# Key rows for the memory by DMA transposes of two fp16 halves, and memory products two row groups later

## The chip, the cores and the metric

One core of a Trainium2 chip runs the kernel. The metric is device microseconds of one execution, the median of three runs. The core has TensorE (PE, with weight loads as PEld), VectorE (DVE), ScalarE (ACT), GpSimd (POOL), and SyncE (SP), whose queue issues all DMAs of this kernel.

## The reference

A gated sum of an attention branch with a memory and a GeGLU feed-forward branch, over one sequence of 2048 rows of 576 numbers (32 heads of 18). The attention branch goes through four segments of 512 rows; each reads a memory that the earlier segments' keys and values built up:

```python
phi = lambda t: jnp.where(t > 0, t + 1.0, jnp.exp(t))
...
for s in range(N):
    qs, ks, vs = q[:, :, s], k[:, :, s], v[:, :, s]
    logits = jnp.einsum("bhqd,bhkd->bhqk", qs, ks) * scale + mask
    a_dot = jnp.einsum("bhqk,bhkd->bhqd", _softmax(logits), vs)
    pq = phi(qs)
    num = jnp.einsum("bhld,bhde->bhle", pq, M)
    den = jnp.einsum("bhld,bhd->bhl", pq, z)[..., None] + 1e-6
    outs.append(g * num / den + (1.0 - g) * a_dot)
    pk = phi(ks)
    M = M + jnp.einsum("bhld,bhle->bhde", pk, vs)
    z = z + jnp.einsum("bhld->bhd", pk)
...
b = (gelu(x @ w_gate) * (x @ w_up)) @ w_down
return gx * (o @ wo) + (1 - gx) * b
```

The change touches only the lines of M and z: how phi(k), computed with columns in the partitions, gets its rows (tokens) into the partitions for the product with v.

## The kernel before

Numbers are carried as pairs of fp16, a high half and the low rest, and products are sums of three half products. The program has two parts. The first, up to about 208 us, makes q, k and v for the four segments, the gate and the memory; the second interleaves the feed-forward branch with the attention heads and ends with the output product. The change lies in the first part.

Segment s (0 to 3) consists of **row groups** (s from 1 on; four groups q of 128 tokens) and nine **column products** j (`project`; j 0 to 3 queries, 4 shared by queries and keys, 5 to 8 keys; 128 columns by 512 tokens each). p = s - 1 is the segment whose keys are put into the memory while s runs.

A row group makes v of 128 tokens in two halves (`vrows`, then `put_rows`: ACT writes the high half of `vstage`, DVE the low one), and, between them, calls `key_rows(p, q - 1)`. From segment 2 on it ends with `recall` (queries times memory, in the two `st` banks of PSUM; `put_recall` on DVE frees them), and then with `memorize(p, q - 1)`, fifteen small products into the banks `U` and `pv`. Group 3's `key_rows` comes after the last group, its `memorize` after column product 0, and `keep_memory` folds the sum into `bd` at column product 1.

A column product is put away by `put_columns` one step later: ACT writes the high half of `stage`, then Relu and Exp into `expm`; DVE makes `phi` from PSUM, POOL adds `expm`; DVE makes the low half of `stage`, and SP writes both to DRAM. The columns of j = 8 are put away in row group 0 of the next segment. Beside j = 5 to 8, `next_x` makes the fp16 halves of the next segment's x (`high_x` on ACT, L205; `low_x` on DVE, L210 and L215).

`key_rows` turns 128 tokens of the five key blocks of `phi` (four blocks into one bank, L714, the fifth into bank `V`, L715) by TensorE transposes against an fp32 identity; ACT scales the result from PSUM into the high half of `krow` (L720), and DVE makes the low half (L724).

PE, ACT, DVE and POOL run in the order in which the code calls them; `finish_later` sends out work that a helper has put into the list `later`. SP's queue is set in order by the framework, by the place of each DMA's data, and SP waits in order too. The buffers of a pool (`stage` 4, `expm` 2, `phi` 9, `vstage` 6) come free when their last reader is done.

Of the kernel before, what the change touches and what calls it, by code (L numbers as in the profile page):

```python
# [45 lines left out]
def kernel(ctx: ExitStack, tc: tile.TileContext, xs, wqk, wv, wo, wgu, wd, beta, out):  # L46
# [472 lines left out]
    kmc = cst.tile([P, 3, 4], F32, name="kmc")  # L519
# [6 lines left out]
    with tc.tile_pool(name="prj", bufs=2, side="right", reuse_waits="tile") as pp:  # L526
# [10 lines left out]
        W, phi, vst, kr, mem = {}, {}, {}, {}, {}  # L537
# [15 lines left out]
        def square_sum(o, r, on_act):  # L553
            if on_act:
                junk = flat(pa.tile([P, 2, KT * P], F16, name="kjunk", bufs=1)).bitcast(BF16)
                act.activation(junk[:, : r.shape[1]], r, AF.Square, accum_out=o)
            else:
                sum_squares(o, r)
# [22 lines left out]
        later, held = [], []  # L581
# [31 lines left out]
        def put_columns(s, j, pr):  # L613
            hf, c = divmod(s, 2)
            st = pp.tile([P, 2, L], F16, name="stage", bufs=4)
# [4 lines left out]
            if with_phi:  # L620
                e = pp.tile([P, L], F32, name="expm", bufs=2)
                f = phi[s, j] = pp.tile([P, L], F32, name="phi", bufs=9)
                act.activation(e, pr, AF.Relu, scale=nal[:, s, i // 2 : i // 2 + 1])
                act.activation(e, e, AF.Exp, scale=-1.0)

            def rest():
                if with_phi:
                    dve.tensor_scalar(f, pr, al[:, s, i : i + 1], 0.0, OP.mult, OP.max)
                    (dve if j == 8 and s == 0 else pool).tensor_tensor(f, f, e, OP.add)
                if j < 8 or s == 3:  # L630
                    words()
# [9 lines left out]
        def put_rows(s, q, b, pv, unit, a):  # L641
# [3 lines left out]
            if b == 0:  # L645
                st = vst[s, q] = pa.tile([P, H, VC], F16, name="vstage", bufs=6)
# [62 lines left out]
        def key_rows(s, q):  # L709
            ka, kb = bank("G") if s else bank("st", 2), bank("V")  # L710
            tok = slice(q * P, (q + 1) * P)

            for i in range(4):
                pe.transpose(ka[:, i * P : (i + 1) * P], phi[s, 4 + i][:, tok], ident)  # L714
            pe.transpose(kb[:, :P], phi[s, 8][:, tok], ident)  # L715
            k = kr[s, q] = krow[q % 2]
            sc = kmc[:, s, 1:2]
            parts = (slice(0, 448), ka[:, 64:]), (slice(448, D), kb[:, :P])
            for o, r in parts:
                act.activation(k[:, 0, o], r, AF.Copy, scale=sc)  # L720

            def low():
                for o, r in parts:
                    dve.scalar_tensor_tensor(k[:, 1, o], r, sc, k[:, 0, o], OP.mult, OP.subtract)  # L724

            later.append(low)

# [1101 lines left out]
```

## Time and profile before

| what | value |
|---|---|
| median of 3 runs | 1556.35 us (1556.0 to 1557.39) |
| the profiled execution, first to last instruction | 1553.8 us |
| granted TensorE clock, mean | 1.000 |
| first part, to the first feed-forward product | about 208 us |
| row groups of segments 1, 2, 3 begin at | 51.3, 98.8, 150.9 us |
| column products of segments 1, 2, 3 begin at | 70.2, 122.5, 174.8 us |

The profile gives the span of the profiled execution only; the runs were timed without it, and their median lies 2.55 us above that span. Rows of a timeline read: start in us, length in us, engine, line, operation, what is written <- what is read, shapes, count, and in brackets how long the engine stood idle before and who released it. Rows of stretches give the busy time of PE, PEld, DVE, ACT and POOL in that order, then TensorE's granted clock, the share of DMA engines busy, and GB/s.

### The profile page before, as it was taken

To read this page: it belongs to the slowest core of one execution; us is meant where nothing else is said; L and a number is where in the kernel's file an instruction comes from. 1 tells how busy PE (TensorE), PEld (TensorE's weight loads), DVE (VectorE), ACT (ScalarE), POOL (GpSimd) and SP (SyncE) were. 2 spreads that over 40 slices of the span, in tenths; PEclk is the share of its full clock that TensorE was granted. 3 is DMA by queue.
4 is the path that set the end of the run, shared out by engine and by line. 5 is a ranking of instruction groups with operands and counts; after the bars stand their busy time and mean duration, and the time that the engine had idled before them with its cause. 6 is when DMAs were issued, how large, how long until landed. Compare 5 with 4: busy or idle time off the path is not lost.

```text
span 1553.8 us, 33925 instructions
## 1 busy us (share of the span) xinstructions
PE 1548.4 (100%) x12195; PEld 955.7 (62%) x12196; DVE 1229.3 (79%) x3198; ACT 1183.7 (76%) x2037; POOL 1305.8 (84%) x1313
## 2 busy tenths in 40 slices
PE   9999999999999999999999999999999999999999
PEld 5665655666666566666666665666666666666577
DVE  6788976778878887878788887878787878887665
ACT  7567544888888888888888888888888888876421
POOL 3544778899898999989899989898999989899597
PEclk9999999999999999999999999999999999999999
DMA  7533341667768687778777878878687878774654
GB/s 254 195 127 125 132 150 34 122 126 140 133 131 141 130 144 130 144 126 137 132 136 126 140 139 136 135 140 151 127 138 133 144 128 141 130 136 99 120 118 138
DMA packets 472601, 210.14 MB, mean 135 GB/s; under 512 B 427632, under 2 KB 437360, under 8 KB 471920
## 3 DMA queue, kind: packets, MB, share of 16 engines
q1 hardware_dynamic: 472432, 207.97, 67.6%
q8 instruction: 96, 1.57, 0.4%
q14 instruction: 73, 0.60, 0.1%
HBM read 92.03 MB, written 27.26 MB: 77 GB/s over the span
## 4 chain that ended last, share of the span: by engine, by line
PE 94%; POOL 3%; ACT 2%; DVE 1%; issue 1%; POOLq 0%
PE dn L1228 27%; PE U L1268 22%; PE V L1268 12%; PE pv L1183 4%; PE G L385 3%; PE st L447 3%; PE dn L454 2%; PE U L1275 2%; PE dn L385 1%; PE U L447 1%; PE V L1280 1%; PE G L1280 1%; PE st L1137 1%; PE G L447 1%; PE st L1669 1%; PE V L1275 1%
## 5 line engine op out<-in xcount | busy, mean ns | idle before, releaser
L1228 PE MATMUL dn<-paird,hh 128*128 128x288 f16 x3396 | 476.5, 286 | 0.2
L1164 POOL TENSOR_TENSOR pf<-pf,ph 128x512 f16<-128x512 f32 (+1 forms) x256 | 359.2, 1403 | 94.6 <-ACT ph L1163 83.6
L1228 PEld LDWEIGHTS <-hh 128*128 128x128 f16 x3456 | 332.2, 98 | 139.1 <-issue 18.1
L1268 PEld LDWEIGHTS <-pairg 128*128 128x128 f16 x2616 | 244.0, 98 | 254.8 <-issue 18.3
L1236 DVE SCALAR_TENSOR_TENSOR acc<-dn,ev,acc 128x288 f32<-128x288 f32 x534 | 274.4, 515 | 51.4 <-PE dn L1228 42.9
L1153 ACT ACTIVATE pf<-pf,mb,esc 128x512 f32<-128x512 f32 (+3 forms) x512 | 293.0, 642 | 5.2
L1268 PE MATMUL U<-xt,pairg 128*128 128x512 f16 x864 | 209.9, 379 | 0.2 <-DVE gl L1459 0.2
L1268 PE MATMUL U<-x,pairg 128*128 128x512 f16 x840 | 204.1, 379 | 0.0
L426 POOL TENSOR_TENSOR pairg<-raw,pairg 128x640 f16<-128x640 f32 (+2 forms) x144 | 176.2, 1239 | 3.0 <-ACT pairg L418 1.5
L1163 ACT ACTIVATE ph<-pf 128x512 f16<-128x512 f32 (+1 forms) x256 | 172.4, 720 | 0.0
L1255 POOL TENSOR_TENSOR hh<-gl,hh 128x512 f16<-128x512 f32 x144 | 164.4, 1163 | 7.5 <-ACT hh L1254 7.5
L1140 DVE CUSTOM_DVE_ANT_0 pf<-st,mask 128x512 f32<-128x512 f32 (+1 forms) x256 | 157.2, 614 | 0.0
L418 ACT ACTIVATE pairg<-raw 128x640 f16<-128x640 f32 (+2 forms) x144 | 89.3, 647 | 56.6 <-POOL raw L410 36.2
L1258 ACT ACTIVATE gl<-gl,sc 128x512 f32<-128x512 f32 x144 | 97.2, 716 | 40.7 <-DVE gl L1505 30.1
L303 POOL TENSOR_SCALAR raw<-raw,sc 128x640 f32<-128x640 f32 x72 | 118.7, 1663 | 0.0
L1459 DVE COPY gl<-U 128x512 f32<-128x512 f32 x72 | 49.8, 692 | 85.4 <-PE U L1268 74.9
L1150 ACT ACTIVATE mb<-mx,esc 128x4 f32<-128x4 f32 x128 | 37.5, 293 | 103.4 <-DVE mx L1140 103.4
L1140 DVE CUSTOM_DVE_ANT_0 pf<-dn,mask 128x256 f32<-128x256 f32 (+1 forms) x192 | 67.2, 375 | 55.3 <-PE dn L1137 55.3
L1268 PE MATMUL V<-xt,pairg 128*128 128x512 f16 x432 | 105.7, 381 | 0.0
L1268 PE MATMUL V<-x,pairg 128*128 128x512 f16 x432 | 104.8, 378 | 0.0
L1254 ACT ACTIVATE hh<-gl 128x512 f16<-128x512 f32 x144 | 82.6, 616 | 16.0 <-DVE gl L1250 15.8
L1183 PEld LDWEIGHTS <-pt 128*128 128x128 f16 x2560 | 83.4, 96 | 12.3
(354 smaller groups left out, 2971.1 us busy)
## 6 DMA issues: line engine op xcount, KB each, us to landing
raw<-in_wgu_dram SPq DMA_DIRECT2D x36, 640.0 KB
rawd<-in_wd_dram SPq DMA_DIRECT2D x36, 288.0 KB
qk<-stage SPq DMA_DIRECT2D x36, 256.0 KB
qt<-qk SPq DMA_DIRECT2D x128, 72.0 KB
kt<-qk SPq DMA_DIRECT2D x128, 72.0 KB
vp<-vstage SPq DMA_DIRECT2D x16, 296.0 KB
vt<-vp SPq DMA_DIRECT2D x16, 296.0 KB
qt<-qk SPq DMA_DIRECT2D x128, 36.0 KB
```

Of the source, the lines that this page charges most:

```text
L303: pool.tensor_scalar(r, r, scl[f // 2][0][:, 0:1], None, OP.mult)
L426: pool.tensor_tensor(spot(f, *p, 1), raw_g[f][:, p[0] : p[1]], spot(f, *p, 0), OP.subtract)
L1140: dve.tensor_tensor_reduce(prob[a][:, COL[qi] : COL[qi] + (qi + 1) * P], out[qi], mask[:, L - (qi + 1) * P :], 1.0, -3e38, OP.add, OP.max, ...
L1153: act.activation(r, r, AF.Exp, bias=b[:, qi : qi + 1], scale=esc[:, 0, c : c + 1])
L1163: act.activation(h[:, cols], p[:, cols], AF.Copy)
L1164: pool.tensor_tensor(p.bitcast(F16)[:, cols], p[:, cols], h[:, cols], OP.subtract)
L1183: pe.matmul(ov, pr[:, 10 * i + COL[qi] // P + kb], v[:, 4 * e + kb, c0 : c0 + VC], start=kb == 0 and i == 0, stop=kb == qi and i == 1)
L1228: pe.matmul(o[:, :NH], hh[:, a, q * P : (q + 1) * P], w[:, b, n * NH : (n + 1) * NH], start=i == 0, stop=i == 5)
L1236: dve.scalar_tensor_tensor(av, o[:, :NH], ev, av, OP.mult, OP.add)
L1255: pool.tensor_tensor(hh[:, 1], t, hh[:, 0], OP.subtract)
L1258: act.activation(t, o, AF.Gelu_apprx_tanh, scale=scl[f // 2][0][:, 2 + c : 3 + c])
L1268: pe.matmul(o, w[:, i, (a + k) * P : (a + k + 1) * P], x[:, b + k], start=start and k == 0 and i == 0 and b == h, stop=k == 1 and i == 1, ...
```

## The change

The transposes leave TensorE. `phi` of key columns is scaled by its power of two when it is made (`kmc` columns 2 and 5 as the factor, and columns 3 and 4, its logarithm, as the bias of Exp). For each of the five key blocks of segments 0 to 2, `turn_keys` has ACT copy `phi` to fp16 into the first half of the block's own `expm` buffer, POOL write the rest phi - high into the second half, and SP turn each half by one DMA transpose of 128 (64 for block 4) columns by 512 tokens into `krow`, which now holds all four groups.

```diff
-        def key_rows(s, q):
...
-            for i in range(4):
-                pe.transpose(ka[:, i * P : (i + 1) * P], phi[s, 4 + i][:, tok], ident)
-            pe.transpose(kb[:, :P], phi[s, 8][:, tok], ident)
...
-                act.activation(k[:, 0, o], r, AF.Copy, scale=sc)
...
-                    dve.scalar_tensor_tensor(k[:, 1, o], r, sc, k[:, 0, o], OP.mult, OP.subtract)
+        def turn_keys(at_once=False):
+            while to_turn:
+                s, j, e = to_turn.pop(0)
+                h = slice(64 if j == 4 else 0, P)
+                f, w = phi[s, j], e.bitcast(F16).rearrange("p (i t) -> p i t", i=2)
+                act.copy(w[h, 0], f[h])
+                def low():
+                    pool.tensor_tensor(w[h, 1], f[h], w[h, 0], OP.subtract)
+                    for i in range(2):
+                        sp.dma_start(krow[:, :, i, max(0, (j - 4) * P - 64) : (j - 3) * P - 64], w[h, i], transpose=True)
+                low() if at_once else lows.append(low)
```

In `put_columns` the copy of the block before stands between Relu and Exp, and its subtraction behind the sum of the present block; the sum of block 8 is on DVE in every segment:

```diff
                 act.activation(e, pr, AF.Relu, scale=nal[:, s, i // 2 : i // 2 + 1])
-                act.activation(e, e, AF.Exp, scale=-1.0)
+                turn_keys()
+                if j >= 4 and s <= 2:
+                    act.activation(e, e, AF.Exp, scale=-1.0, bias=kmc[:, s, 4:5] if j == 4 else kmc[:, s, 3:4])
+                else:
+                    act.activation(e, e, AF.Exp, scale=-1.0)
...
-                    (dve if j == 8 and s == 0 else pool).tensor_tensor(f, f, e, OP.add)
+                    (dve if j == 8 else pool).tensor_tensor(f, f, e, OP.add)
+                while lows:
+                    lows.pop(0)()
+                if keys:
+                    to_turn.append((s, j, e))
```

In the row groups and column products:

```diff
                         put_rows(s, q, 0, *pv)
                         if s == 3 and q == 0:
+                            for i in range(2):
+                                squares(0, 1, i, act_square)
+                        turn_keys(True)
+                        if s == 3 and q == 0:
                             norm_x(3, bank("V"))
-                        if q:
-                            key_rows(p, q - 1)
...
-                        if q:
-                            memorize(p, q - 1)
+                        if q > 1:
+                            memorize(p, q - 2)
                     finish_later()
-                    key_rows(p, 3)
...
-                    if s and j == 0:
+                    if s and j < 2:
                         finish_later()
-                        memorize(p, 3)
+                        memorize(p, j + 2)
+                    if j == 2 and s < 3:
+                        key_scale(s)
...
-                    if s and j == 1:
+                    if s and j == 2:
                         keep_memory(p)
```

Besides: `stage` has 3 buffers, `expm` 4, `phi` 8, `vstage` 7; `krow` also serves as scratch for squares and for `keep_memory`; `key_scale` is called at j = 2 of its own segment, with five small instructions more; the POOL scalings `outscale` are called one at j = 5, 6 and 7 each instead of all at j = 4 or 5, and `mix_scale` in segment 2; of the `form_sums` subtractions in the row groups of segments 2 and 3, two and one move from DVE to POOL, and their ACT part comes later in the group.

ACT and DVE at the border of segments 1 and 2, where the last column product of segment 1 is put away and row group 0 of segment 2 runs (`expm`, `stage`, `phi` belong to the column products, `vstage` to the rows of v, `mo` to `put_recall`). Before, ACT:

```order
L618 ACTIVATE stage<-G 128x512
L623 ACTIVATE expm<-G,nal 128x512
L624 ACTIVATE expm<-expm 128x512
L651 ACTIVATE vstage<-dn 128x16x18 x2
L651 ACTIVATE vstage<-U 128x16x18
```

and now:

```order
L632 ACTIVATE stage<-G 128x512
L637 ACTIVATE expm<-G,nal 128x512
L588 CAST expm<-phi 128x512
L640 ACTIVATE expm<-expm,kmc 128x512
L675 ACTIVATE vstage<-dn 128x16x18
L588 CAST expm<-phi 128x512
L675 ACTIVATE vstage<-dn 128x16x18
L675 ACTIVATE vstage<-U 128x16x18
```

The first cast reads `phi` of block 7, the second that of block 8; each now stands ahead of a `vstage`. DVE at the same place now has the sum of block 8 ahead of the first `vstage` and of `put_recall`:

```order
L648 TENSOR_SCALAR phi<-G,kmc 128x512
L649 TENSOR_TENSOR phi<-phi,expm 128x512
L678 SCALAR_TENSOR_TENSOR vstage<-dn,vstage 128x16x18
L658 SCALAR_TENSOR_TENSOR stage<-G,stage 128x512
L678 SCALAR_TENSOR_TENSOR vstage<-dn,vstage 128x16x18
L680 TENSOR_SCALAR gate<-dn,al 128x1
L718 COPY mo<-st 128x19
```

Before, that sum was on POOL. SP's queue from block 4 of segment 0 to the first rows of segment 1 (`qk` and `vp` are written to DRAM, `raw` is read for the x of segment 2). Before:

```order
L635 DMA qk<-stage 128x2x512
L161 DMA raw<-in_xs_dram 128x1024
L635 DMA qk<-stage 128x2x512
L161 DMA raw<-in_xs_dram 128x1024
L657 DMA vp<-vstage 128x1184
L635 DMA qk<-stage 128x2x512
L657 DMA vp<-vstage 128x1184
L635 DMA qk<-stage 128x2x512
```

Now, the second half of the same stretch:

```order
L593 DMA_TRANSPOSE krow<-expm 128x4x128
L681 DMA vp<-vstage 128x1184
L593 DMA_TRANSPOSE krow<-expm 128x4x128 x2
L161 DMA raw<-in_xs_dram 128x1024
L593 DMA_TRANSPOSE krow<-expm 128x4x128 x2
L659 DMA qk<-stage 128x2x512
L681 DMA vp<-vstage 128x1184
```

Ten transposes now stand between these transfers, in the order in which their halves are made; the last two rows of transposes are blocks 7 and 8, with a load of x between them.

More of the change, by code (lines that the diff above doesn't have):

```diff
@@ L6 @@
 from concourse._compat import with_exitstack
-from concourse.masks import make_identity
 F32 = mybir.dt.float32
@@ L753, in keep_memory @@
                 else:
-                    m = flat(pa.tile([P, 2, KT * P], F16, name="kjunk", bufs=1)).bitcast(F32)[: o.shape[0], : o.shape[1]]
+                    o, d, k = (t.rearrange("p (a b) -> p a b", a=2) for t in (o, d, k))
+                    m = krow[: o.shape[0], 0, :, : 2 * o.shape[2]].bitcast(F32)
                     dve.scalar_tensor_tensor(m, o, sm[: o.shape[0]], k, OP.mult, OP.mult)
@@ L795 @@
                 pool.memset(t, 1e-30)
-            krow = [pa.tile([P, 2, KT * P], F16, name=f"krow{i}", bufs=1) for i in range(2)]
-            for t in krow:
-                pool.memset(t[:, :, D:], 0.0)
+            krow = pa.tile([P, 4, 2, KT * P], F16, name="krow", bufs=1)
+            pool.memset(kmc[:64, :, 4:5], 0.0)
             bdm = pa.tile([P, KT, 8 * MC], BF16, name="bdm", bufs=1)
@@ L858, in next_x @@
                         add_squares(c, (3,))
-                if j == (4 if c > 1 else 5):
-                    for i in range(3):
-                        outscale(c, i)
                 if 5 <= j < 8:
@@ L1051 @@
                     finish_later()
+                    if s < 3 and 5 <= j < 8:
+                        outscale(s + 1, j - 5)
                     if (s, j) == (1, 3):
```

75 lines of the change are left out of this document (36 added, 39 removed).

## The prediction

> **What bounds the kernel now.** I read the page first, then who TensorE waited for over the whole run, then the timeline around the transposes. The page's first lines:
>
> ```profile
> span 1553.8 us, 33925 instructions
> PE 1548.4 (100%) x12195; PEld 955.7 (62%) x12196; DVE 1229.3 (79%) x3198; ACT 1183.7 (76%) x2037; POOL 1305.8 (84%) x1313
> ```
>
> TensorE is busy for 1548.4 of 1553.8 us, and the whole list of what it waits for before is three short rows:
>
> ```profile
> PE G L783 <- POOL wst L779: 1.0, 1, 1.0
> PE dn L457 <- DVE wv L128: 0.4, 1, 0.4
> PE U L1268 <- DVE gl L1459: 0.2, 1, 0.2
> ```
>
> So the kernel is TensorE's queue from end to end. An instruction taken off that queue is worth its place in the queue; any new wait of TensorE is lost in full. The sum is therefore (places removed) minus (waits added). I work against the profiled span, 1553.8 us; the median of the runs, 1556.35, is 2.55 us above it, and I carry that difference unchanged.
>
> **What leaves TensorE.** One call of `key_rows`, in segment 1 and row group 1, and behind it a place in the same timeline where one chain of `vrows` follows the other with nothing between:
>
> ```profile
> 56.32 0.29 PE L457 MATMUL U<-wv,x 128*128 128x288 f16 x1
> 56.45 0.60 PE L714 MATMUL st<-ident,phi 128*128 128x128 f32 x4
> 56.88 0.27 PE L715 MATMUL V<-ident,phi 128*128 128x128 f32 x1
> 56.99 1.64 PE L454 MATMUL dn<-wv,x 128*128 128x290 f16 x12
> ...
> 52.88 0.29 PE L457 MATMUL dn<-wv,x 128*128 128x288 f16 x1
> 53.00 1.64 PE L454 MATMUL dn<-wv,x 128*128 128x290 f16 x12
> L715 PE MATMUL V<-ident,phi x12: 272/273/273, 56.9 to 174.7; 128*128 128x128 f32 x12
> ```
>
> Matmuls overlap, so starts count, not durations. From the last matmul of a chain to the first of the next it is 0.67 us with five transposes and 0.12 us without: 0.55 us a call. The last row shows twelve calls (one `kb` transpose each): 12 x 0.55 = **6.6 us removed**. The memory products stay the same fifteen per row group; moving them two groups later changes no count. Nothing waited for these transposes long, so their removal opens no further wait of TensorE.
>
> **What is added, on engines beside TensorE.** Fifteen blocks of key columns (five in each of segments 0 to 2) get one ACT copy to fp16, one POOL subtraction and two DMA transposes. The nearest rows of the same shapes:
>
> ```profile
> L1254 ACT ACTIVATE hh<-gl 128x512 f16<-128x512 f32 x144 | 82.6, 616 | 16.0 <-DVE gl L1250 15.8
> L1255 POOL TENSOR_TENSOR hh<-gl,hh 128x512 f16<-128x512 f32 x144 | 164.4, 1163 | 7.5 <-ACT hh L1254 7.5
> ```
>
> That is 0.6 us on ACT and 1.2 us on POOL a block. ACT and DVE lose the copies and subtractions of `key_rows`, so in sum they are relieved. What matters is where the new work stands: in the ACT queue the copy of block 7 stands between Relu and Exp of block 8, and it waits for POOL's sum of block 7; block 8's own sum is now a DVE instruction that waits for that Exp; and ahead of the next `vstage` on ACT stands the copy of block 8, which waits for that sum. In the rows before of segment 2 these read:
>
> ```profile
> 100.80 1.27 POOL L629 TENSOR_TENSOR phi<-phi,expm 128x512 f32<-128x512 f32 x1 [1.50 <-ACT expm L624]
> ...
> 100.17 0.63 ACT L624 ACTIVATE expm<-expm 128x512 f32<-128x512 f32 x1
> 100.71 0.41 ACT L651 ACTIVATE vstage<-dn 128x288 f16<-128x288 f32 x1
> ...
> 53.85 0.87 DVE L629 TENSOR_TENSOR phi<-phi,expm 128x512 f32<-128x512 f32 x1
> ...
> 103.01 0.45 DVE L654 SCALAR_TENSOR_TENSOR vstage<-dn,vstage 128x288 f16<-128x288 f32 x1
> 103.62 0.18 DVE L694 COPY mo<-st 128x19 f32<-128x19 f32 x1
> 104.96 0.82 DVE L705 TENSOR_TENSOR mo<-st,rden 128x396 f32<-128x396 f32 x2
> ...
> 107.41 1.37 PE L683 MATMUL st<-bd,phi 128*128 128x152 f32 x10
> ```
>
> POOL's sum of block 7 ends at 102.07; before, ACT was through with Exp at 100.8 and did not care. Now: copy 0.6, Exp 0.6, DVE sum 0.87 (the row at 53.85, the one such sum that was on DVE), copy 0.6, `vstage` 0.41, its low half and the gate column 0.6: 105.75. Only then does `put_recall` of group 0 start; it took 103.62 to 105.78, 2.16 us, so it ends near 107.9 and frees both `st` banks. TensorE wants them for the next `recall` at 107.41 - 0.55 = 106.86. **A new wait of 1.0 us** in segment 2.
>
> The same in segment 3, where two squares of `raw` now stand ahead of that copy:
>
> ```profile
> 152.74 1.27 POOL L629 TENSOR_TENSOR phi<-phi,expm 128x512 f32<-128x512 f32 x1 [1.37 <-DVE phi L628]
> ...
> 154.59 0.74 ACT L556 ACTIVATE kjunk<-raw 128x640 bf16<-128x640 f32 x1 [0.57 <-DMA raw<-in_wgu_dram]
> 155.45 0.74 ACT L556 ACTIVATE kjunk<-raw 128x640 bf16<-128x640 f32 x1
> ...
> 157.12 0.17 DVE L694 COPY mo<-st 128x19 f32<-128x19 f32 x1
> 158.45 0.82 DVE L705 TENSOR_TENSOR mo<-st,rden 128x396 f32<-128x396 f32 x2
> ...
> 159.76 1.37 PE L683 MATMUL st<-bd,phi 128*128 128x152 f32 x10
> ```
>
> 154.0 + copy 0.6 + Exp 0.6 + `vstage` 0.4 = 155.6; the two squares 1.6 (154.59 to 156.19 by these rows): 157.2; copy 0.6, `vstage` 0.4, low half and gate 0.6: 158.8; `put_recall` 2.15: 160.95. TensorE comes at 159.76 - 0.55 = 159.2. **A new wait of 1.7 us.** If POOL's sum or `raw` is 1 us later, both waits grow by it; if the earlier blocks run ahead, they vanish. Bounds: 0 to 2.5 us and 0 to 4 us.
>
> **The transposes by DMA** have no row of this size. The nearest are the probability transposes, 128 rows by 1280 against 512 here:
>
> ```profile
> L1169 SPq DMA_TRANSPOSE pt<-ph x128: 1252/1372/3217, 273.6 to 1420.7; - x128
> ...
> 55.75 0.37 SPq L635 DMA_DIRECT2D qk<-stage  x1
> ...
> 44.00:60.00 16.00, 16.00 (x126) 11.61 (x125) 13.98 (x30) 10.71 (x21) 13.69 (x13) 1.00 0.98 315
> 600.00:1000.00 400.00, 400.00 (x3329) 244.26 (x3328) 325.87 (x888) 341.11 (x580) 363.50 (x352) 1.00 0.78 135
> ...
> 51.73 1.27 POOL L629 TENSOR_TENSOR phi<-phi,expm 128x512 f32<-128x512 f32 x1 [1.84 <-DVE phi L628]
> 58.72 0.80 PE L737 MATMUL U<-vstage,krow 128*128 128x152 f16 x9
> 59.68 1.63 PE L454 MATMUL dn<-wv,x 128*128 128x288 f16 x12
> 63.67 0.80 PE L737 MATMUL U<-vstage,krow 128*128 128x152 f16 x9
> ```
>
> One occupies SP's queue for 1.37 us; for 512 columns between 0.55 (in proportion) and 1.37 (fixed); I take 1.0, between them, since nothing here decides. In the two rows of stretches the last column but one is the DMA share: at 600 to 1000 us the engines are 0.78 busy for 135 GB/s, at 44 to 60 us 0.98 busy for 315 GB/s. So traffic with such transposes moves fewer bytes per busy time, 173 GB/s when full; a block's two, 0.26 MB, would then fill the engines for 1.5 us, and those of segment 0 fall into the stretch that is full already. I let a landing be 1 to 4 us. TensorE wants them all, complete, for `memorize(0, 0)` at 63.67 - 1.1 (two calls of `key_rows`) - 0.96 (the memory products that leave group 1, 58.72 to 59.68) = 61.6. Block 7's sum ends at 53.0; copy, Exp and block 8's sum as above give 55.1, its copy 55.7, its subtraction, behind block 7's, about 57.5. Ten transposes and eight plain transfers go through SP from 44 us on: at 1.0 and 0.37 us 13 us, so SP is just through. Two issues and a landing later it is 60.5 to 63.5. **I take a wait of 1.0 us**, bounds 0 to 4. In segments 2 and 3 `recall` gives the transposes 1.2 us more a group: no wait.
>
> **The lock between DVE and POOL** can make all three worse:
>
> ```profile
> 43.60 1.27 DVE L210 SCALAR_TENSOR_TENSOR x<-raw,xsc,x 128x1024 f16<-128x1024 f32 x1
> 95.19 2.01 DVE L210 SCALAR_TENSOR_TENSOR x<-raw,xsc,x 128x1024 f16<-128x1024 f32 x1
> 94.84 1.28 POOL L629 TENSOR_TENSOR phi<-phi,expm 128x512 f32<-128x512 f32 x1 [1.91 <-DVE phi L628]
> ```
>
> The same DVE instruction takes 1.27 us with POOL idle and 2.01 us when POOL is inside a sum that began just before it. The Trainium skill (SBUF — State Buffer, "SBUF: two separate sides") states an exclusive lock on a shared port pair; these rows agree (0.74 us more). Each segment's blocks 4 to 8 now have a second POOL instruction of 1.2 us beside DVE's `low_x`. One collision more, about half an instruction, per segment: 0.5 us, thrice, **1.5 us**, bounds 0 to 3.5.
>
> **Sum.** -6.6 + 1.0 + 1.7 + 1.0 + 1.5 = -1.4 us: span 1552.4, time **1555.0 us**.
>
> **Rivals.** 1. *The waits hide* (faster). POOL's scale instructions of `outscale` are spread out and `expm` has four buffers, so the earlier blocks may run ahead and the ACT chain end in time. Only about 1.5 us of wait remain: 1556.35 - 5.1 = 1551.3. Against it stands DVE (third number, 90 to 102 us), which is busy for 11.87 of 12 us there, so that block 7 cannot come sooner than DVE lets it:
>
> ```profile
> 90.00:102.00 12.00, 12.00 (x69) 6.51 (x68) 11.87 (x16) 9.30 (x16) 6.67 (x8) 1.00 0.62 191
> ```
>
> 2. *The transposes land late* (slower). SP takes its queue in order, and between the transposes stand the writes of `stage` (one buffer fewer) and the loads of x. At 1.37 us an issue, ten make 13.7 us, SP is still issuing at 61 us in segment 0, and every `memorize` of the first groups waits: 4 us in segment 0, and with 1.5 in each later one and the upper bounds of the ACT chain (2.5 and 4) less what overlaps (2): 11.5 - 6.6 = +4.9: 1561.2. It decides when landing comes 4 us after the last subtraction. The Trainium skill (VectorE: DVE Perf Modes, "The three transpose paths") points this way: it gives 390 ns for a 128x128 on TensorE, 1309 ns by DMA, and advises TensorE where PSUM will do. By that price 36 blocks a segment would be 47 us, and TensorE would stand for tens of us. The trace disagrees: here one instruction of ten such blocks leaves SP in 1.37 us, and TensorE's queue, not a transpose's own duration, is what costs.
>
> 3. *The change does not do what it says*: transposes left on TensorE. In the order of the changed program none is left; no chance.
>
> **How the numbers follow.** Near balance, waits between 3.5 and 9.7 us: 0.44. Waits hidden, rival 1: 0.32. Late transposes, rival 2: 0.24. A measurement can tell about 0.2%, 3.1 us, so faster means below 1553.2 and slower above 1559.5. The range leaves out about a tenth at each end: from nearly all of the 6.6 us kept (1550.5) to just short of rival 2's full price (1560.8).
>
> **What would show it.** No L714 or L715 row, and TensorE's chains 0.12 us apart in the row groups. In TensorE's list of waits: `recall` on `put_recall` (DVE) in group 1 of segments 2 and 3, about 1 and 1.7 us; the first `memorize` of segment 1 on a DMA, about 1 us. ACT's copies idle on POOL's `phi`. The prediction is wrong if that list stays below 3 us (then 1551), if a DMA or SP heads it with over 4 us, or if waits appear beyond 205 us, where I expect the same times shifted.

## The result, and the profile after

| | before | after |
|---|---|---|
| median of 5 runs each | 1556.35 us | 1569.84 us |
| ratio of the runs, 95% interval | | 1.0083 [1.0071, 1.0095] |
| profiled execution, first to last instruction | 1553.8 us | 1567.9 us |
| granted TensorE clock, mean | 1.000 | 0.996 |

The change makes the kernel 13.5 us slower. The prediction was 1555.0 us, in a range of 1550.5 to 1560.8. (One execution of the experiment k1 below took 5611.21 us; its median is that of its other four.) The page of the changed kernel:

```profile
span 1567.9 us, 33879 instructions
PE 1548.7 (99%) x12135; PEld 951.4 (61%) x12136; DVE 1228.5 (78%) x3188; ACT 1182.0 (75%) x2028; POOL 1330.6 (85%) x1327
```

TensorE has 60 instructions fewer (twelve calls of five transposes) and is busy no less: 1548.7 against 1548.4 us. Idle are 19.2 us of its span instead of 5.4. The list of what TensorE waits for had three rows; now it reads (us in total, times, longest):

```profile
PE pv L742 <- DMA krow<-expm: 3.0, 1, 3.0
PE dn L99 <- DVE vstage L678: 2.9, 1, 2.9
PE st L707 <- DVE mo L729: 2.4, 2, 1.5
PE dn L454 <- DVE gate L680: 2.0, 2, 1.0
PE dn L454 <- DVE vstage L678: 1.8, 2, 1.2
PE U L742 <- DMA krow<-expm: 1.1, 1, 1.1
PE G L795 <- POOL wst L791: 1.0, 1, 1.0
PE dn L457 <- DVE wv L128: 0.5, 1, 0.5
PE dn L707 <- DVE mo L729: 0.3, 1, 0.3
```

L742 is `memorize`, L707 `recall`, L454 a chain of `vrows`, L99 the column sums of `scales(0)` in segment 3. All but the last three rows are new; of the three, two stood in the list before, and 0.3 us fall at the end of the first part. Where the time goes is read from the first product of each stage of TensorE's timeline (row groups of segment 1, its columns, and so on):

```profile
52.76 1.64 PE L454 MATMUL dn<-wv,x 128*128 128x288 f16 x12 [1.02 <-DVE gate L680]
74.81 1.46 PE L447 MATMUL dn<-x,wp 128*128 128x512 f16 x6
104.38 1.63 PE L454 MATMUL dn<-wv,x 128*128 128x288 f16 x12
128.98 2.32 PE L447 MATMUL dn<-x,wp 128*128 128x512 f16 x10
158.56 1.63 PE L454 MATMUL dn<-wv,x 128*128 128x288 f16 x12
187.45 1.89 PE L447 MATMUL dn<-x,wp 128*128 128x512 f16 x8
```

Before, these stood at 51.29, 70.15, 98.77, 122.49, 150.88 and 174.82. Each segment has four `key_rows` fewer in its rows (2.2 us) and one `memorize` of 0.96 us moved into its columns, so the growth of a stage plus 3.16 us is what its rows lost:

| stage | growth, us | lost in it, us | waits listed there | slower clock (next section) |
|---|---|---|---|---|
| up to the rows of segment 1 | 1.5 | 1.5 | 1.0 | |
| rows of segment 1 | 3.2 | 6.4 | 4.0 | 1.5 |
| rows of segment 2 | 0.9 | 4.0 | 3.3 | |
| rows of segment 3 | 5.0 | 8.1 | 4.7 | 2.9 |
| columns of segments 1 and 2 | 0.9, 1.2 | 0, 0.2 | | |

20.2 lost less 6.6 removed is 13.6 of the 14.1 us. The listed waits and the slower clock are 17.4 of the 20.2. Part of the rest comes from how a wait is listed: from the modelled end of the last product, while products overlap. At the first wait of segment 1 two products start 1.30 us apart (51.46 and 52.76) where 0.12 is usual, so 1.18 us are lost for 1.02 listed. What remains was not traced. Behind 205 us nothing new waits for more than 0.3 us.

### The profile page after: what moved, and what is told of

It is laid out like the page before. It is cut to its first block, busy times and chain, and to the rows that moved or that the text cites. A ratio compares the mean times of both kernels' runs of the same rounds, so it can differ in the third digit from the quotient of the medians.

```text
span 1567.9 us, 33879 instructions
## 1 busy us (share of the span) xinstructions
PE 1548.7 (99%) x12135; PEld 951.4 (61%) x12136; DVE 1228.5 (78%) x3188; ACT 1182.0 (75%) x2028; POOL 1330.6 (85%) x1327
## 4 chain that ended last, share of the span: by engine, by line
PE 88%; POOL 5%; DVE 3%; ACT 2%; issue 1%; DMA 1%; SPq 0%; POOLq 0%; DVEq 0%; ACTq 0%
PE dn L1239 27%; PE U L1279 22%; PE V L1279 12%; PE pv L1194 4%; PE G L385 3%; PE U L1286 2%; PE dn L385 1%; PE st L447 1%; PE G L1291 1%; PE V L1291 1%; PE st L1148 1%; PE st L1680 1%; PE V L1286 1%; PE G L1286 1%; PE dn L454 1%
```

## The experiments

All times are medians beside runs of the kernel before on the same chip (1555.9 to 1556.7 us). The ratios differ from those of the medians by up to 0.0004, so a difference of under 1 us between two experiments decides nothing. Line numbers of an experiment differ from those of the changed kernel by a few.

### Segment 1: the queue of SP, and the clock behind a wait

What TensorE waits for in the rows of segment 1 is issued by SP. In the changed kernel all thirty transposes on SP's queue (min/median/max in ns), POOL's subtraction of block 8, SP's rows around the last transposes of segment 0, TensorE's rows that wait for them, and a chain of segment 3:

```profile
L593 SPq DMA_TRANSPOSE krow<-expm x30: 1177/1214/2406, 44.7 to 172.1; - x30
...
58.54 1.16 POOL L591 TENSOR_TENSOR expm<-phi,expm 128x512 f16<-128x512 f32 x1 [1.10 <-ACT expm L588]
...
58.65 1.23 SPq L593 DMA_TRANSPOSE krow<-expm  x1
59.97 0.53 SPq L681 DMA_DIRECT2D vp<-vstage  x1
60.59 2.53 SPq L593 DMA_TRANSPOSE krow<-expm  x2
63.17 1.14 SPq L161 DMA_DIRECT2D raw<-in_xs_dram  x1
64.40 2.52 SPq L593 DMA_TRANSPOSE krow<-expm  x2
...
65.03 0.60 PE L742 MATMUL U<-vstage,krow 128*128 128x152 f16 x3 [1.05 <-DMA krow<-expm]
68.61 0.91 PE L742 MATMUL pv<-vstage,krow 128*128 128x152 f16 x6 [2.98 <-DMA krow<-expm]
69.33 2.70 PE L454 MATMUL dn<-wv,x 128*128 128x288 f16 x12
...
175.14 2.71 PE L454 MATMUL dn<-wv,x 128*128 128x288 f16 x12
```

SP works through its queue without a gap; the subtraction of block 8 is done at 59.70 (58.54 + 1.16), but its transposes leave only at 64.40. And behind the wait the same twelve products that take 1.63 us elsewhere take 2.70, and 2.71 behind the waits of segment 3. So two theories: SP's time per transpose, and the granted clock.

**one_dma**: one transpose a block for both halves.

```diff
-                    for i in range(2):
-                        sp.dma_start(krow[:, :, i, max(0, (j - 4) * P - 64) : (j - 3) * P - 64], w[h, i], transpose=True)
+                    sp.dma_start(krow.rearrange("p i q c -> p (i q) c")[:, :, max(0, (j - 4) * P - 64) : (j - 3) * P - 64], e.bitcast(F16)[h], transpose=True)
...
-            krow = pa.tile([P, 4, 2, KT * P], F16, name="krow", bufs=1)
+            krow = pa.tile([P, 2, 4, KT * P], F16, name="krow", bufs=1)
```

> One DMA transpose a block for the high and the low half together, 15 instructions instead of 30; the bytes, the casts and the subtractions stay. Theory SP (each transpose holds SP's queue about 1.2 us whatever its size, so ten of them put the last one of segment 0 behind the first memorize of segment 1): the time between the starts of two transposes stays near 1.2 to 1.6 us though each moves twice the columns, the wait of TensorE for krow in the rows of segment 1 (3.0 + 1.1 us in the changed kernel) falls to 0 to 1 us, the slower clock behind it goes too, and the time falls by 3 to 5.5 us, to 1564.5 to 1567 us. Rival DMA (the moving of the bytes is what is late): a transpose of twice the columns takes twice as long on SP's queue or to land, and wait and time stay within 1 us (1569 to 1571 us). In segments 2 and 3 both expect the waits unchanged.

Measured: 1563.53 us, ratio to before 1.0047 [1.0032, 1.0062]; 6.3 us less than the changed kernel (5.6 by the ratios). The wait for `krow` is 1.7 us instead of 4.1, and behind it the clock stays full. (In segment 3, behind pauses of 2.86 and 0.82 us, it still falls: twelve products take 3.08 us there.) Twice the columns hold SP's queue for 1.30 instead of 1.21 us:

```profile
L592 SPq DMA_TRANSPOSE krow<-expm x15: 1194/1303/3062, 50.2 to 165.6; - x15
```

Theory SP holds, the rival DMA falls: the bytes are the same. The wait fell a little less than expected and the gain was a little larger.

**fill**: products that nothing reads, where TensorE waited longest.

```diff
+                        if (s, q) == (1, 2):
+                            o = bank("pv")
+                            for _ in range(22):
+                                pe.matmul(o, onesb, mask, start=True, stop=True)
```

and twelve of them ahead of `scales(0)` in segment 3.

> The changed kernel with matrix products that nothing reads, put where TensorE waits longest: 22 of 128x512 ahead of the first memorize of segment 1, 12 ahead of the column sums of the squares in segment 3 (some 4.7 and 2.6 us at full clock). Theory CLOCK (a wait of about 3 us makes the granted clock fall to half for some us behind it): the granted clock no longer falls behind these two places, the chain that took 2.70 us behind the first of them takes 1.63 again, and the time stays equal or falls by up to 4 us although the fillers add up to 3 us more than the waits that they cover: 1566 to 1570 us. Rival (the clock falls for another reason, as the power of the products before): the chains stay at 2.7 us behind the same products, and the fillers add 2 to 4 us, 1572 to 1574 us.

Measured: 1567.04 us, 1.0066 [1.0051, 1.0081]; 2.8 us less than the changed kernel, with 34 products more. The chains behind the two places:

```profile
68.76 1.63 PE L454 MATMUL dn<-wv,x 128*128 128x288 f16 x12
167.52 1.65 PE L454 MATMUL dn<-wv,x 128*128 128x290 f16 x12 [0.83 <-DVE gate L680]
```

In the changed kernel they took 2.70 and 1.97 us, and in segment 3 the recall and the chain behind took 2.71 each instead of 1.37 and 1.63. So the pauses themselves cost some 1.5 + 2.9 us beyond their length. Theory CLOCK holds.

### Segments 2 and 3: the ring of ACT and POOL

In segment 2 of the changed kernel, POOL, ACT, DVE and TensorE around the start of the row groups at 104.38 (L649 is a sum, L591 the subtraction of a low half, L588 the fp16 copy):

```profile
101.83 2.02 POOL L591 TENSOR_TENSOR expm<-phi,expm 64x512 f16<-64x512 f32 x1
104.20 1.81 POOL L649 TENSOR_TENSOR phi<-phi,expm 128x512 f32<-128x512 f32 x1
105.97 1.16 POOL L591 TENSOR_TENSOR expm<-phi,expm 128x512 f16<-128x512 f32 x1
107.64 1.27 POOL L649 TENSOR_TENSOR phi<-phi,expm 128x512 f32<-128x512 f32 x1
...
106.04 0.62 ACT L588 CAST expm<-phi 128x512 f16<-128x512 f32 x1 [1.28 <-POOL phi L649]
108.95 0.62 ACT L588 CAST expm<-phi 128x512 f16<-128x512 f32 x1 [0.61 <-POOL phi L649]
110.09 0.41 ACT L675 ACTIVATE vstage<-dn 128x288 f16<-128x288 f32 x1
111.73 0.62 ACT L588 CAST expm<-phi 128x512 f16<-128x512 f32 x1 [1.23 <-DVE phi L649]
...
110.22 1.47 DVE L649 TENSOR_TENSOR phi<-phi,expm 128x512 f32<-128x512 f32 x1 [0.67 <-ACT expm L640]
...
112.12 1.64 PE L454 MATMUL dn<-wv,x 128*128 128x290 f16 x12 [1.20 <-DVE vstage L678]
115.48 1.45 PE L707 MATMUL st<-bd,phi 128*128 128x152 f32 x10 [1.48 <-DVE mo L729]
```

The reader is to see a ring. The copy of block 6 waits for POOL's sum of block 6; Exp of block 7 stands behind that copy; the sum of block 7 needs that Exp, and stands on POOL behind the low half of block 5; the copy of block 7 waits again. The first `vstage` begins 5.7 us after the row groups; before it was 1.9 us (100.71 against 98.77).

**cast_behind**: the copies stand behind Exp of the next block, that of block 8 behind both `vstage`. **both**: this and one_dma.

```diff
-                turn_keys()
...
                     act.activation(e, e, AF.Exp, scale=-1.0)
+                turn_keys()
...
-                        turn_keys(True)
...
                         put_rows(s, q, 1, *pv)
+                        turn_keys(True)
```

> The fp16 copies of the key blocks move back in ACT's order: behind Exp of the next block instead of ahead of it, and the one of block 8 behind both vstage copies of row group 0. Theory ACT (the copies wait for POOL's and DVE's sums and hold up the vstage copies behind them): the waits of TensorE for dn and st in segments 2 and 3 (L454, L99, L707: 2.9 + 2.4 + 2.0 + 1.8 us) fall to 2 to 5 us in sum, the clock loss of 3 us in segment 3 goes for the most part, and the time falls by 4 to 8 us; the wait for krow in segment 1 may grow by 1 to 2 us since the transposes start later. Rival LOCK (DVE and POOL instructions lengthened by each other, or the buffers of phi and stage, make the sums late): the same waits stay within 1.5 us in sum, and the time stays at 1568 to 1572 us.

> One transpose a block, and the copies moved back in ACT's order. If SP and ACT are both right and act in different segments, the gains add up: 7 to 13 us less than the changed kernel, 1557 to 1563 us. If SP alone: 1564.5 to 1567. If ACT alone: 1562 to 1566. If neither: 1568 to 1572.

Measured: cast_behind 1568.10 us, 1.0072 [1.0055, 1.0089]; both 1565.36 us, 1.0055 [1.004, 1.007]. The waits of segments 2 and 3 fell only from 8.0 to 6.2 us in cast_behind, less than ACT asked for and a little more than LOCK allowed; the time lies in LOCK's range. With one_dma beneath it the move lost 1.8 us: the waits of segments 2 and 3 fell from 7.0 to 5.3, but since the copies of segment 0 came later too, the wait for `krow` was 3.7 us, against 1.7 in one_dma, and the clock fell behind it. So in both the gain in segments 2 and 3 and the loss in segment 1 hid each other, and its time, which lies where SP alone or ACT alone would put it, shows neither.

**no_low** goes on from one_dma and leaves out the subtraction in segments 1 and 2, so only the high half is transposed there; **no_keys** leaves out the copies and transposes as well.

```diff
+                    if s:
+                        sp.dma_start(krow[:, 0, :, max(0, (j - 4) * P - 64) : (j - 3) * P - 64], w[h, 0], transpose=True)
+                        return
                     pool.tensor_tensor(w[h, 1], f[h], w[h, 0], OP.subtract)
...
                 s, j, e = to_turn.pop(0)
+                if s:
+                    continue
```

The first addition is no_low's, the second stands only in no_keys.

> One transpose a block as in one_dma (1563.5 us), and in segments 1 and 2 the subtraction that makes the low half is left out (ten POOL instructions of 1.16 to 2.03 us; the products with the low half read old values), so only the high half is transposed there. Theory POOL (its queue, with each low half ahead of the next block's sum, makes the sums late for which ACT and DVE wait): the waits of TensorE in segments 2 and 3 (1.8 + 1.5 + 2.9 + 0.8 us in one_dma) fall to 0 to 3 us, the clock loss of about 3 us in segment 3 goes, and the time falls by 5 to 9 us, to 1554.5 to 1558.5 us. Rival ACT (the copies in its order are enough): these waits stay within 1.5 us in sum, the time within 2 us.

> As no_low, and in segments 1 and 2 the fp16 copies on ACT and the transposes are left out too (the memory products read the keys of segment 0 again); what stays of the change there is the sum of block 8 on DVE, the scale columns, and the later memory products. Theory POOL: nothing more to gain than no_low gains, within 1.5 us. Rival ACT: the time falls by 6 to 10 us against one_dma, to 1553.5 to 1557.5 us, and by most of that against no_low. Rival LOCK/DVE (the sum of block 8 on DVE and the moved columns are what delays vstage): both kernels stay above 1560 us with waits of 4 us and more in segments 2 and 3.

Measured: no_low 1558.83 us, 1.0016 [1.0006, 1.0025], 4.7 us less than one_dma; no_keys 1558.31 us, 1.0011 [1.0002, 1.0021]. The waits in segments 2 and 3 went from 7.0 to 4.1 and 3.65 us. Theory POOL comes near in time (4.7 where 5 was the least expected), though its waits were to fall to 3 us or less; once the low halves are gone, the copies are worth 0.5 us, which is within the noise. But 3.65 us of waits stay without any of the key work, so part of the lateness comes from what else the change did. Candidates are the sum of block 8 on DVE ahead of `vstage`, TensorE itself, which comes 0.55 us earlier to a recall, and POOL's additions beside `put_recall` (k8 below moves some of them); the first two were not tried apart.

**early2** goes on from one_dma and converts the next x two blocks earlier in segments 1 and 2, **early2_mix** also moves the copies of these segments behind Exp.

```diff
-                    next_x(s + 1, j)
+                    next_x(s + 1, j, 2 if s else 0)
```

> One_dma with the conversion of the next x (squares, scale, high half on ACT, low half on DVE) two column blocks earlier in segments 1 and 2, where ACT and DVE wait for TensorE's blocks: nothing is left out. Theory PACE (in blocks 4 to 8 ACT, DVE and POOL each have 3.3 to 3.6 us of work per block against 3.03 us of TensorE, and the lateness adds up until block 8): waits in segments 2 and 3 fall from 7 us to 1 to 4 us and the clock loss goes: time 1555 to 1559.5 us. Rival POOL (its queue alone sets the lateness, and x has no part on POOL): waits stay above 5 us and the time within 2 us of one_dma, 1561.5 to 1565.5. The lock between DVE's low half of x and POOL's low half of block 4 (2.03 us instead of 1.16) should go by either.

> As early2, and in segments 1 and 2 the fp16 copies stand behind Exp of the next block, that of segment 2's block 8 behind both vstage copies; segment 0 keeps them where the change put them. PACE and ACT both right: waits in segments 2 and 3 fall to 0 to 2 us, time 1553 to 1557 us. PACE alone: like early2 within 1 us. ACT alone: 1560 to 1563 us.

Measured: 1562.85 us, 1.0044 [1.0028, 1.0061], and 1562.56 us, 1.004 [1.0025, 1.0054]: within 1 us of one_dma. The waits in the rows of segments 2 and 3 went from 7.0 to 5.95 and 3.65 us, but new ones of 1.7 and 1.8 us came in the columns of segment 2, where TensorE needs bank `U` and `keep_memory` on DVE was late. PACE is not shown: early2 came out as its rival said, early2_mix in the range of ACT alone, and what came free in the rows was given back in the columns. The low half of block 4 took 1.16 us here, as expected (its row stands further down).

**k1** to **k4** go on from one_dma. All have x one block earlier and its scales on POOL one block earlier (`outscale`), and `memorize(0, 0)` behind the first chain of row group 3; k2 adds the copies behind Exp in segments 1 and 2 (that of block 8 behind both `vstage`), k3 the low halves one place further back, k4 both.

```diff
                         pv = vrows(s, q, 0)
+                        if (s, q) == (1, 3):
+                            memorize(p, 0)
...
-                while lows:
+                while len(lows) > (s > 0 and j < 8):
                     lows.pop(0)()
```

> One transpose a block (one_dma, 1563.5 us), and three moves that leave nothing out: the next x is converted one column block earlier in segments 1 and 2 (two blocks earlier had put a wait of 1.7 us before the third block of the columns), its output scales on POOL one block earlier too, and in segment 1 the first memory product stands 1.6 us later, behind the first chain of row group 3. Theory POOL (in segments 2 and 3 what counts is how early POOL is through with its queue; no_low had 1558.8 us): POOL has 2.3 us less in blocks 5 to 7, the waits of segments 2 and 3 fall by 2 to 5 us, that on krow by 1.5 us: 1556.5 to 1560 us. Rival (POOL's order, not its amount: each low half still stands ahead of the next sum): only the krow wait goes, 1561 to 1562.5 us.

> k1 with the fp16 copies behind Exp of the next block in segments 1 and 2. If ACT's order still counts beside POOL's: 1 to 2.5 us less than k1. If POOL alone sets the lateness: within 1 us of k1, or up to 1 us more, since the low halves start later.

> k1 with each low half of segments 1 and 2 one place further back in POOL's queue, behind the sum after next (the same instructions, all of them). Theory POOL by its order: the sums of blocks 6 and 7 come 1.2 us earlier each, the copies on ACT stop waiting for them, the waits in segments 2 and 3 fall by 2 to 4 us against k1: 1554 to 1557 us. Rival (amount of work alone): within 1 us of k1. A buffer may bite: Relu of block 8 then needs the transpose of block 4 to be done, and starts later if that takes over 2 us from POOL's end.

> k3 and k2 together. If both orders count: the lowest of the four, 1553 to 1556 us. If POOL's order alone: within 1 us of k3.

Measured: 1566.69, 1565.26, 1569.26 and 1567.86 us (1.007 [1.0056, 1.0083], 1.006 [1.0046, 1.0074], 1.0083 [1.007, 1.0097], 1.0077 [1.0065, 1.009]), all above one_dma, k2 not clear of noise. The wait for `krow` is gone in k1 to k3 (0.3 us in k4), as expected of the later product. But with x one block earlier TensorE waits 1.6 and 2.4 us for bank `U`, which `keep_memory` frees, in the columns of segments 1 and 2. And nothing came of it in the rows: in segment 2 of k1, 1.9 us for `vstage` and 1.5 for the recall, where one_dma has 1.8 and 1.5. In k3, the worst, a chain of `vrows` waits 2.9 us. In these runs less work on POOL and later low halves do not shorten the waits. k2 is 1.4 us below k1, but in the two profiles 1.7 us of difference come from the clock at one place (last section).

**k5** keeps from k1 only the later `memorize`, puts `outscale` ahead of block 4's sum and the norm of x at column 3; **k6** adds the copies behind Exp in segments 1 and 2, as k2; **k7** puts `form_sums` of segment 3 back where it was before the change.

```diff
-            NORMS = {(1, 2): 0, (1, 5): 1, (2, 5): 2}
+            NORMS = {(1, 2): 0, (1, 3): 1, (2, 3): 2}
...
-                turn_keys()
+                if s == 0:
+                    turn_keys()
...
                     act.activation(e, e, AF.Exp, scale=-1.0)
+                turn_keys()
```

> One transpose a block (one_dma, 1563.5 us), the first memory product of segment 1 behind the first chain of row group 3, and of the moves in k1 only those that take nothing in front of the columns 0 to 3: x is converted where the change had it, its output scales stand on POOL ahead of the sum of block 4 instead of between the sums of blocks 5 to 7, and the norm of x (a product and a reduction that DVE waits for ahead of phi of block 4) two blocks earlier. Theory POOL-ORDER (what stands between the sums on POOL, scales of 0.28 to 1.25 us and low halves of 1.16 to 2.03 us, makes them late): the krow wait goes (-1.7 us), no wait comes at the third block of the columns, the waits of 3.3 and 3.7 us in segments 2 and 3 fall by 2 to 4 us together: 1558 to 1560 us. Rival LOOP (ACT's copy of a block waits for POOL's sum, whose Exp stands behind the copy before it: a ring of 2.6 to 3.4 us per block that no other order on POOL shortens): only the krow wait goes, 1561.5 to 1562.5 us.

> k5 with the fp16 copies of segments 1 and 2 behind Exp of the next block, which cuts the ring of ACT and POOL. LOOP: 1.5 to 3 us less than k5. POOL-ORDER: within 1 us of k5.

> k6 with the partial sums of acc in segment 3 where they were before the change (the first on POOL behind group 0, the others on DVE). Theory LOCK (POOL's 2.3 us additions make DVE's small steps of put_recall and of the scales 1.05 and 0.84 us longer there): the waits in segment 3 fall by 0.5 to 1.5 us against k6. Rival: DVE's own 1.2 us additions take the same place, within 0.5 us of k6, or slower.

Measured: k5 1562.33 us, 1.0036 [1.0024, 1.0049]; k6 1559.04 us, 1.0017 [1.0008, 1.0026]; k7 1560.32 us, 1.0028 [1.0018, 1.0039]. k5 is where LOOP put it and above the range of POOL-ORDER, though the medians alone do not part the krow wait from the rest. Its waits in segments 2 and 3 did not fall (7.9 us, 7.0 in one_dma). k6 gains 3.3 us by the copies' place alone, more than LOOP asked for, and these waits are 4.8 us. k7 is 1.3 us slower, so moving these additions back gains nothing. In k6, segment 2 (row groups from 97.98 on), ACT and TensorE:

```profile
100.03 0.60 ACT L588 CAST expm<-phi 128x512 f16<-128x512 f32 x1
102.36 0.60 ACT L588 CAST expm<-phi 128x512 f16<-128x512 f32 x1
102.87 0.72 ACT L676 ACTIVATE vstage<-dn 128x288 f16<-128x288 f32 x2
103.68 0.62 ACT L588 CAST expm<-phi 128x512 f16<-128x512 f32 x1
...
107.86 1.45 PE L708 MATMUL st<-bd,phi 128*128 128x152 f32 x10 [1.28 <-DVE mo L730]
```

None of these copies waits any more, and both `vstage` are out 5.6 us after the row groups began; in the changed kernel the second was out after 8.3 us (112.25 + 0.42 against 104.38).

**k8** has the second pair of squares in segment 3 behind `vstage`, and the four POOL additions for the norm of x in segment 2 at column 0; **k9** also has `scales(0)` behind the recall of group 1; **k10** also the copies of segment 0 behind Exp.

```diff
-                        if s == 3 and q == 0:
-                            for i in range(2):
-                                squares(0, 1, i, act_square)
...
                         put_rows(s, q, 1, *pv)
+                        if s == 3 and q == 0:
+                            for i in range(2):
+                                squares(0, 1, i, act_square)
```

> k6 (1559.0 us) with the two squares of raw in segment 3 behind vstage of group 0 instead of ahead of it, and in segment 2 the four additions for the norm of x on POOL moved from group 0 to the first column block. Theory ACT-ORDER (the wait of 0.8 for the gate column and part of the 1.5 us for the column sums come from vstage behind the squares): the gate wait goes, that of the column sums stays at 1 to 1.5 us. Theory LOCK (POOL's additions stretch one DVE step of put_recall from 0.19 to 1.00 us): the recall wait of segment 2 falls from 1.3 to about 0.5 us. Both: 1557 to 1558.3 us. Neither: 1558.5 to 1559.5.

> k8 with the column sums of the squares (and the scaling that follows) behind the recall of group 1 instead of ahead of its second chain, so that TensorE has 3 us of other work before it needs the squares. The wait of 1.5 us and the clock loss of some 2 us behind it go: 1554 to 1556 us, at or a little below the kernel before (1556.3). Rival: the scaling on POOL ends 3 us later and the conversion of the weights in segment 3 or the end of the rows waits for it: 1557 us or more.

> k9 with the copies of segment 0 behind Exp too. The wait of 1.0 us at the start of segment 1's rows (vstage behind a copy that waits for POOL) goes, the transposes start up to 1 us later: 0.5 to 1 us less than k9. Rival SP: the krow wait comes back with 1 to 3 us, and the time is 0 to 2 us above k9.

Measured: k8 1557.74 us, 1.001 [1.0001, 1.0018]; k9 1558.83 us, 1.0012 [1.0003, 1.0021]; k10 1558.65 us, 1.0012 [1.0003, 1.0021]. k8 has the lowest time of all, 12.1 us below the changed kernel and still 1.0 us above the runs of before beside it (1556.73); k9 and k10 are not clear of it, nor it of k6. The recall wait of segment 2 fell from 1.3 to 0.5 us, as LOCK had it (rows below). The gate wait of segment 3 stayed, at 0.6 instead of 0.8 us, against ACT-ORDER. k9 missed. Its time lies in its rival's range, but not for the reason that the rival named: the wait for the squares went and the clock stayed full, and the next things in the queue waited instead. Rows of k9's list:

```profile
PE st L708 <- DVE mo L730: 2.3, 2, 1.9
PE dn L454 <- DVE vstage L679: 1.4, 1, 1.4
```

k10 neither gained nor lost: the wait of 1.0 us at the start of segment 1's rows stayed, so it does not come from the copies' place on ACT. DVE's low half of x ahead of it, first in the kernel before and then in k10:

```profile
46.05 1.27 DVE L210 SCALAR_TENSOR_TENSOR x<-raw,xsc,x 128x1024 f16<-128x1024 f32 x1
```

```profile
46.59 1.98 DVE L210 SCALAR_TENSOR_TENSOR x<-raw,xsc,x 128x1024 f16<-128x1024 f32 x1
46.22 1.27 POOL L648 TENSOR_TENSOR phi<-phi,expm 128x512 f32<-128x512 f32 x1 [0.21 <-ACT x L205]
47.57 2.03 POOL L591 TENSOR_TENSOR expm<-phi,expm 64x512 f16<-64x512 f32 x1
```

In k10 it is 0.7 us longer: POOL's sum had begun ahead of it. And POOL's low half of block 4, which begins inside it, is longer too. That this makes the wait was not tried.

## Why the prediction was wrong

**The removal was right.** The twelve calls are gone, and where the next row waits for nothing one chain follows the other 0.12 us later. Behind 205 us the work runs as before, only later, as the prediction said.

**The transposes by DMA: the mechanism right, the size wrong.** The prediction took 1.0 us per transpose on SP, between 0.55 (in proportion) and 1.37 (fixed), "since nothing here decides", and a wait of 1.0 us, bounds 0 to 4. The transposes hold the queue for 1.21 us at 512 columns and 1.30 at 1024, so nearly all of it is fixed, and TensorE waited 4.0 us (3.0 + 1.1 in the list, which a DMA heads: the sign that the prediction had named for being wrong). Rival 2 described segment 1 well: it set its point at 4 us from the last subtraction to the landing, and it was 8.9 us (59.70 to 68.61). It was a matter of the queue in order, not of moving bytes: one_dma moved the same bytes. The Trainium skill (VectorE: DVE Perf Modes, "The three transpose paths") gives 1309 ns for a 128x128 by DMA; here eight such blocks leave SP's queue in 1.30 us, so on this queue a price of that size falls on the instruction and not on the block. As predicted, segments 2 and 3 did not wait for transposes.

**The ACT chain: the step that failed.** The prediction began its chain with "POOL's sum of block 7 ends at 102.07", the time of the kernel before, and added the copies behind it. But the copies and low halves of blocks 4 to 6 stand in the same ring, so that sum itself came 1.2 us later against the row groups (4.5 instead of 3.3 us behind their start), DVE's sum of block 8 took 1.47 instead of 0.87, and DVE's low half of the first `vstage`, queued behind that sum, held a bank of `vrows`, which the prediction did not look at. In place of 1.0 us there were 3.3 in segment 2: 1.5 for the recall, where the prediction had 1.0, and 1.8 for the first product chains of `vrows`, which wait for such a low half. In segment 3 two squares stand, as before, ahead of `stage` of block 8, but now behind the late copy of block 6, and `stage` of block 8 begins 4.6 us after the row groups, where it had been 1.0:

```profile
160.38 0.62 ACT L588 CAST expm<-phi 128x512 f16<-128x512 f32 x1 [1.42 <-POOL phi L649]
163.11 0.58 ACT L632 ACTIVATE stage<-G 128x512 f16<-128x512 f32 x1
```

That made 4.7 us of waits in place of 1.7. k6 cut the ring by the place of the copies and gained 3.3 us on k5; no_low cut it by the low halves and gained 4.7 on one_dma. Six pairs of runs differ by the place of the copies in segments 1 and 2 (in two pairs in segment 0 as well), and in each the waits of segments 2 and 3 fell by it, by 0.8 (k4 against k3) to 3.1 us (k6 against k5).

**The lock** of DVE and POOL shows in the rows, and both sides pay. The prediction's row of 1.27 us was not "with POOL idle": POOL's small instruction at 43.83 took 1.11 us there, 0.21 at 41.86, so there it was POOL that waited. POOL's low half of block 4 took 2.02 us beside L210 (the row at 101.83); in early2, where x is converted earlier, it takes 1.16:

```profile
97.51 1.16 POOL L591 TENSOR_TENSOR expm<-phi,expm 64x512 f16<-64x512 f32 x1
```

One small DVE step of the first `put_recall` in segment 2, in k6 and then in k8, where POOL's four additions no longer run beside it:

```profile
106.11 1.00 DVE L728 TENSOR_TENSOR rden<-rden,gh 128x32 f32<-128x32 f32 x1
```

```profile
106.71 0.19 DVE L728 TENSOR_TENSOR rden<-rden,gh 128x32 f32<-128x32 f32 x1
```

The 0.8 us of this step are the 0.8 us by which the recall wait fell. In k6 it began inside one of POOL's additions (105.92 to 107.07) and ended with it; in the kernel before the same step, at 104.73, fell between two such additions (the first ends at 104.74, the next begins at 104.82) and took 0.19. So some tenths of a us decide which side pays, and how much. What the lock costs in all cannot be set apart from the waits above, so the term of 1.5 us stays unmeasured.

**What no step had.** The slower clock behind the waits, about 4.4 us, and the 1.5 us up to the rows of segment 1. And the range ended below rival 2's full price, although both doubtful terms rested on times of the kernel before that the change itself moves.

What stays open: the last 1 us (0.2 to 2.8 by the interval) between k8 and the kernel before. The largest waits left in k8 are 1.7 us for the column sums of segment 3 and 1.6 for gate columns, and behind the former the clock falls (twelve products in 3.08 us); k9 took both of these away in segment 3 and gained nothing. No version beat the kernel before.

## What to carry to other kernels

When TensorE has no gap, work taken off it pays only if the engines that receive it are through before its next use; trace the ring of engine queues from the first new instruction on, not from the last one of the old trace. Count DMA transposes by instruction on the issuing queue, and make few large ones. A copy that waits for another engine belongs behind, not ahead of, what that engine needs next.

## What was not expected of the hardware

The granted clock fell to about half for 2 to 7 us behind some pauses of TensorE (in the changed kernel its mean is 0.57 from 68 to 72 us, and 0.62 from 169 to 178), and the length of the pause does not decide it. Two kernels with the same pause of 2.39 us (k1, then k2; fourteen products that take 3.19 us at full clock):

```profile
138.61 4.88 PE L447 MATMUL U<-x,wp 128*128 128x512 f16 x14 [2.39 <-DVE krow L760]
...
138.04 3.20 PE L447 MATMUL U<-x,wp 128*128 128x512 f16 x14 [2.39 <-DVE krow L762]
```

In k3 a pause of 2.88 us passed without it; in early2_mix two pauses of 1.11 and 0.83 us with one short product between brought it on. The Trainium skill (TensorE: Matmul & The Clock Gate, "Part 1: The HAM clock gate") has the clock go by an activity window of about 3.4 us that runs free of the kernel, and halve it after an idle window. A free-running window fits that the same pause does both; but no pause here is as long as such a window (the longest is 3.28 us, in the run `both`), so by these runs less than an idle window is enough. How much was not measured.
